# Loading the value weights whole and first, and making three pairs of values before the queries and keys of step 0

## The chip, the cores and the metric

The kernel runs on one core of a Trainium2 chip. The metric is the device time of one execution in microseconds (us). The engines are TensorE (PE, with its weight loads shown apart as PEld), VectorE (DVE), ScalarE (ACT), GpSimd (POOL) and SyncE (SP). SP computes nothing here: it issues most of the DMAs, in the order of the program. All DMAs are carried by the same 16 DMA engines.

## The reference

Four blocks follow each other, each on a layer norm of the 2048 x 512 input and added to it: attention with a recurrent memory (A), a dense block (B), A again, B again. Everything is bfloat16.

```python
def _A_ref(x, mem0, Wq, Wk, Wv, Wo, seg_len):   # seg_len 32, M = 8 memory rows, H = 32 heads of 128
    mem = mem0
    for s in range(n_seg):                      # 64 segments
        h = jnp.concatenate([mem, xs], axis=1)  # 8 memory rows + 32 tokens
        q, k, v = (jnp.einsum('btd,dhe->bhte', h, W) for W in (Wq, Wk, Wv))
        scores = jnp.where(mask, jnp.einsum('bhqe,bhke->bhqk', q, k) * scale, -1e9)
        o = jnp.einsum('bhqk,bhke->bhqe', _softmax(scores), v)
        o = jnp.einsum('bhte,hed->btd', o, Wo)
        mem = o[:, :M, :]                       # the next segment's memory
        outs.append(o[:, M:, :])
def _B_ref(x, w1, w2):                          # 512 -> 1376 -> 512
    return jnp.maximum(x @ w1, 0) @ w2
x = x + _A_ref(_layernorm(x), ...); x = x + _B_ref(_layernorm(x), ...)   # and both once more
```

The memory rows make the segments a chain: a segment needs the output of the one before it.

## The kernel before

**Steps.** The kernel runs 68 steps. Step k does segment k of the first attention and, four steps behind it, segment k - 4 of the second one; the dense blocks of earlier segments run beside them. Steps 0 to 3 have the first attention alone. Inside a step the 32 heads are done in two halves of 16: queries and keys (`qk`, in batches of 6, 6 and 4 heads), scores, softmax; then the probabilities are turned, the values are weighted (`weighted_v`), and the output product with Wo gives the new memory rows (`output_mem`, `new_memory`), with which the next step starts.

**Order.** The instructions of PE, DVE, SP and POOL run in the order in which the program emits them (a manual schedule); ACT's order is chosen by the framework. An instruction that waits therefore holds everything behind it on its engine.

**Head.** Before the steps, `load_xb(0)` and the weights are issued on SP. Each of Wq, Wk and Wv (4.19 MB, 128 partitions x 4 x 4096 columns) comes in two halves of 2.1 MB, one for each half of the heads, by `load_w`: x0, Wq first half, mem0, x1, Wk first half, Wv first half, and then in `load_rest` x2, the three second halves, Wo in five parts (4.19 MB) and x3. `xbs[n]` holds 128 rows of input. Its layer norm is `moments_x` (statistics on DVE, the power on POOL) and `normalize` (DVE); `inputs_T(n)` turns it with four PE transposes into a PSUM tile and copies that to `xT0[n]` with ACT. `tokens_in` puts the tokens of a step into `HT` (the moving or stationary operand of all products), and a copy on POOL puts the tokens of a step into `HTm`, beside the memory rows.

**Values.** There are four kinds. `values_first(ii)` gives the values of segment 0's memory and tokens: for each half of the heads two PSUM tiles of eight matmuls, the first copied to `Vs` by ACT, the second by DVE, two copies each. `memory_values` makes the values of the memory rows (and of 16 rows of a later segment that ride along), `values_second` those of segment 1, and `values0(p, n)` those of the pair of segments 2 and 3 of every 128 input rows (p odd; n = 0, 2, 4, 6 stand for a quarter of the heads each): eight matmuls into one PSUM tile, an ACT copy to a staging tile, a store to DRAM by SP, from where a later step loads them. In step 0 the staging tiles are slices (`slots`) of the buffers that will hold the dense weights.

The PSUM tiles of `values_first`, `values_second`, `values0` and of the transposes come from one pool of two buffers (`ps_fill`); queries, keys, memory values and turned probabilities share three buffers (`ps_c`). So a tile can be started when the tile two (or three) before it has been copied out.

**Step 0 (`first_step`).** It does the first half of the heads, then values (first half of `values_first`, `memory_values`, `values_second`, and four groups of `values0` for pairs 1 and 3, with the layer norm and transposes of x2 between), then the second half of the heads with two groups of pair 5 between, the second half of the values, and the output, among whose five parts five more groups of `values0` are spread. Groups that are left go into steps 1 (three), 2 (one) and 4 (one) by `values_at`; from step 5 on another rule holds, the same in both kernels.

**Names in the profile.** L241 transposes, L591 queries and keys, L597 and L599 their copies by ACT and DVE, L625 scores, L643 to L664 softmax, L329 `values_first`, L334 its copies, L797 memory values, L354 second values, L310 `values0`, L320 its copy, L232 to L227 the layer norm of an input, L675 turning of probabilities, L701 weighted values, L719 their copies, L633 output product of the memory rows, L849 to L872 the new memory.

Of the kernel before, what the change touches and what calls it, by code (L numbers as in the profile page):

```python
# [7 lines left out]
BF = mybir.dt.bfloat16  # L8
# [14 lines left out]
def kernel(  # L23
# [14 lines left out]
    nc = tc.nc  # L38
# [62 lines left out]
    nc.vector.memset(mem0[:], 0.0)  # L101
    xbs = {}

    def load_xb(n):
        tag, bufs = ("vst", 5) if n in (1, 2, 3) else ("xb", 1)
        xbs[n] = wk.tile([128, Dm], BF, tag=tag, bufs=bufs, name="xb")
        nc.sync.dma_start(out=xbs[n][:], in_=A_x[0, 128 * n:128 * n + 128, :])

    load_xb(0)
    R_tiles = {}  # L110

    def residual(d):
# [17 lines left out]
    PW = H * Dh // 2  # L130
    WO_PARTS = ((0, 8), (8, 16), (16, 24), (24, 28), (28, 32))

    def load_w(W_sb, W_v, pc):
        nc.sync.dma_start(out=W_sb[:, :, pc * PW:(pc + 1) * PW], in_=W_v[:, :, pc * PW:(pc + 1) * PW])

    load_w(Wq_sb, Wq_v, 0)
    nc.sync.dma_start(out=mem0[0:M, :], in_=A_mem0[0, :, :])
    load_xb(1)
    load_w(Wk_sb, Wk_v, 0)
    load_w(Wv_sb, Wv_v, 0)  # L140

    def load_rest():
        load_xb(2)
        load_w(Wq_sb, Wq_v, 1)
        load_w(Wk_sb, Wk_v, 1)
        load_w(Wv_sb, Wv_v, 1)
# [432 lines left out]

    def qk_batch(n, h0, nh, a_lo, a_hi, between=None):
        ncol = (a_hi - a_lo) * L
        res = {}

        for W_sb, nm in (((Wq_sb, "QT"), (Wk_sb, "KT")) if n < 2 else ((Wk_sb, "KT"), (Wq_sb, "QT"))):
            qp = ps_c.tile([128, HB, 2 * L], F32, tag="c")
            for hi in range(nh):
                h = h0 + hi
                for c4 in range(NC4):  # L590
                    nc.tensor.matmul(qp[:, hi, 0:ncol], lhsT=W_sb[:, c4, h * Dh:(h + 1) * Dh],  # L591
                                     rhs=HT[:, c4, a_lo:a_hi, :], start=(c4 == 0), stop=(c4 == NC4 - 1))
            dst = wk.tile([128, nh, 2 * L], BF, tag=f"{nm}{n}", bufs=1, name=nm)
            if nm == "QT":
                if between:
                    between()
                nc.scalar.copy(out=dst[:, 0:nh, a_lo * L:a_hi * L], in_=qp[:, 0:nh, 0:ncol])  # L597
            else:
                nc.vector.tensor_copy(out=dst[:, 0:nh, a_lo * L:a_hi * L], in_=qp[:, 0:nh, 0:ncol])  # L599
            res[nm] = dst  # L600
        return res["QT"], res["KT"]

    BATCHES = ((0, 6), (6, 6), (12, 4))

    def qk(hf, act, between=None, behind=None):
        res = []
        for n, (o, nh) in enumerate(BATCHES):
            res.append((o, nh) + qk_batch(n, 16 * hf + o, nh, act[0], act[-1] + 1, None if n else between))
# [7 lines left out]
        for a in act:  # L616
            nc.vector.tensor_copy(out=sp_tiles[a], in_=maskb2)  # L617

    def scores(qks, act):
        for a in act:  # L620
            sp = sp_tiles[a]
# [13 lines left out]

    last_exp = [None]

    def exponentials(act):
        mxs, ess = {}, {}
        for a in act:  # L640
            sp = sp_tiles[a]
            mxs[a] = wk.tile([128, 8], F32, tag="mx", bufs=2, name="mx")
            nc.vector.tensor_reduce(out=mxs[a][:], in_=sp, axis=AX.X, op=ALU.max)  # L643
        for a in act:
            sp = sp_tiles[a]
# [166 lines left out]
    def block(k, lo, hi):  # L812
        output_x(k - 1, lo, hi)
        groups = values_at(k)
        if split(k):

            rest = [(i, 0, NC4) for i in range(1, len(groups))]
            if k == 1:
                todo = [] if lo == 0 else [(0, 0, 2)] if hi == 16 else [(0, 2, NC4)] + rest
            else:  # L820
                todo = [(0, 0, 2)] if lo == 0 else [(0, 2, NC4)] if hi == 16 else rest
        elif k < 5:
            todo = [(0, 0, NC4)] if k == 4 and lo else []
# [11 lines left out]
    def values_at(k):  # L835


        if k < 5:
            return {1: [(5, 6), (7, 0), (7, 2)], 2: [(7, 4)], 4: [(7, 6)]}.get(k, [])
        if k % 4 != 1 or not has0(k + 1):  # L840
            return []
        groups = [(p, n) for p in range(9, NSEG // 2, 2) for n in range(0, NCH, 2)]
        i = k // 4 - 1
        lo = 3 * min(i, 12) + 4 * max(i - 12, 0)
        return groups[lo:lo + (3 if i < 12 else 4)]
# [39 lines left out]
    def first_step():  # L885


        slots = iter([w1_flat[:, 512 * i:512 * i + 512] for i in range(NC4 * Dff // 512)] +
                     [w2_flat[:, 512 * i:512 * i + 512] for i in range(8)])
        masks(0)  # L890
        with tc.high_priority(offset=PRIO):
            qks = qk(0, [0])
            scores(qks, [0])
            softmax(0, [0], True)
            values_first(0)
            memory_values(0, (next(slots), None), (0,))
            values_second(0, next(slots))
            values0(1, 0, stage=next(slots))
            values0(1, 2, stage=next(slots))
            m = moments_x(2)  # L900
            normalize(nc.vector, xbs[2], xbs[2], m, 0, 128)
            inputs_T(2)
            values0(3, 0, stage=next(slots))
            values0(3, 2, stage=next(slots))
            load_x(1)
            qks = qk(1, [0], between=lambda: values0(5, 0, stage=next(slots)))
            scores(qks, [0])
            softmax(1, [0], True)
            values0(5, 2, stage=next(slots))
            values_first(1)  # L910
            memory_values(0, (None, next(slots)), (1,))
            transpose_p(1)
            tokens_in(1)
            nc.gpsimd.tensor_copy(out=HTm[:, :, 2 * M:32], in_=spare_T(1))
            values_second(1, next(slots))
            pvs = weighted_v([0])
            outputs(0, pvs)
            wo = ps_wo.tile([128, Dm], F32, tag="wo", name="wo")
            for groups, heads in zip((((1, 4),), ((1, 6),), ((3, 4),), ((3, 6), (5, 4)), ()), WO_PARTS):
                for p, n in groups:  # L920
                    values0(p, n, stage=next(slots))
                output_mem(0, wo, *heads)
            new_memory(0, [0], wo)
            output_ride(0)
            prepare(1)
# [225 lines left out]
```

## Time and profile before

| | us |
|---|---|
| median of 3 runs | 1581.19 (1581.16 to 1582.31) |
| the profiled execution | 1581.75 |
| its span | 1580.0 |
| PE busy | 1548.6 (98%) |
| DVE busy | 1277.3 (81%) |
| ACT busy | 734.7 (47%) |
| POOL busy | 349.8 (22%) |
| first matmul of a query | 16.61 after the span's start |
| first matmul of step 1's queries | 51.20 after the span's start |

The span runs from the first to the last instruction of the program; the execution's own time has some 1.7 us around it. "Busy" is the union of the instructions' times on an engine; times in the timeline count from the span's start.

### The profile page before, as it was taken

The page shows a single profiled execution, that of the slowest core. Times are in us where ns is not written, and L with a number is a line of the kernel's source. Part 1 is how long each engine was busy: PE and PEld are TensorE (multiplying, and loading weights), DVE is VectorE, ACT ScalarE, POOL GpSimd, SP SyncE. Part 2 cuts the span into 40 slices and gives each one's busy share as a digit, 9 for nine tenths or more (in the row PEclk, how much of TensorE's full clock was granted, in tenths as well). Part 3 has the DMA queues.
Part 4 walks back from the last instruction along what each step waited for, and adds up shares of the span by engine and source line. Part 5 has one row for each costly group of instructions (what it writes and reads, how often), then busy time and mean ns, then how long its engine had stood idle before and what let it go on. Part 6 is the DMA issues. An engine that isn't in the chain of part 4 may idle for free. (4 is left out here: it accounts for less than half of the span.)

```text
span 1580.0 us, 95139 instructions
## 1 busy us (share of the span) xinstructions
PE 1548.6 (98%) x42866; PEld 1286.3 (81%) x42866; DVE 1277.3 (81%) x3300; ACT 734.7 (47%) x1762; POOL 349.8 (22%) x670
## 2 busy tenths in 40 slices
PE   5899999999999999999999999999999999999998
PEld 3677888888888888888888888988888898888876
DVE  3578888888888888888888888888888888887866
ACT  3435445454544545454454545445454544545433
POOL 2012122222222222222122222212222221222110
PEclk9999999999999999999999999999999999999999
DMA  9734432434353244434433343443443344333331
GB/s 369 246 77 76 87 84 78 81 92 79 78 92 84 78 82 94 80 76 91 84 80 80 99 80 76 88 84 79 77 99 77 72 87 80 82 74 95 75 69 41
DMA packets 222021, 146.26 MB, mean 93 GB/s; under 512 B 123464, under 2 KB 215984, under 8 KB 221616
## 3 DMA queue, kind: packets, MB, share of 16 engines
q1 hardware_dynamic: 218448, 135.96, 38.8%
q8 instruction: 336, 5.51, 1.5%
q0 software_dynamic: 3072, 4.20, 1.1%
q14 instruction: 69, 0.57, 0.1%
q10 hardware_dynamic: 96, 0.03, 0.0%
HBM read 65.41 MB, written 45.35 MB: 70 GB/s over the span
## 5 line engine op out<-in xcount | busy, mean ns | idle before, releaser
L597 ACT CAST QT<-qp 128x480 bf16<-128x480 f32 (+3 forms) x408 | 201.5, 494 | 433.4 <-PE qp L591 433.1
L591 PE MATMUL qp<-HT,Wq_sb 128*128 128x80 bf16 (+1 forms) x8704 | 371.3, 200 | 3.2 <-POOL HT L786 1.2
L591 PEld LDWEIGHTS <-Wq_sb 128*128 128x128 bf16 x8704 | 325.9, 100 | 35.2 <-issue 27.5
L591 PE MATMUL qp<-HT,Wk_sb 128*128 128x80 bf16 (+1 forms) x8704 | 347.3, 199 | 1.7 <-issue 1.3
L591 PEld LDWEIGHTS <-Wk_sb 128*128 128x128 bf16 x8704 | 319.5, 100 | 2.6 <-issue 1.6
L664 POOL TENSOR_TENSOR P_sb<-es,sm 128x320 bf16<-128x320 f32 x185 | 130.8, 721 | 714.8 <-ACT QT L597 299.4
L599 DVE CAST KT<-qp 128x480 bf16<-128x480 f32 (+3 forms) x408 | 220.3, 565 | 36.3 <-PE qp L591 32.9
L643 DVE TENSOR_REDUCE mx<-sp 128x8 f32<-128x320 f32 x256 | 115.1, 487 | 133.1 <-PE sp L625 130.9
L373 PE MATMUL wox<-Wo_sb,OTx 128*64 128x256 bf16 x2880 | 173.6, 273 | 0.0
L373 PEld LDWEIGHTS <-OTx 128*64 128x64 bf16 x2880 | 150.2, 110 | 2.9
L649 ACT ACTIVATE es<-es 128x320 f32<-128x320 f32 x256 | 109.5, 468 | 61.9 <-DVE es L647 61.0
L797 PE MATMUL vm<-Wv_sb,HTm 128*32 128x512 bf16 x2176 | 129.4, 379 | 1.8 <-DVE KT L599 1.0
L354 PE MATMUL v<-Wv_sb,xnT 128*32 128x512 bf16 x2048 | 128.8, 378 | 0.0
L633 PE MATMUL wo<-Wo_sb,OTm 128*32 128x512 bf16 x2144 | 128.6, 380 | 0.0
L659 DVE TENSOR_REDUCE sm<-es 128x8 f32<-128x320 f32 x256 | 117.4, 459 | 13.5 <-ACT es L649 5.0
L617 DVE CAST sp<-maskb 128x320 f32<-128x320 bf16 x256 | 118.3, 483 | 0.0
L647 DVE TENSOR_TENSOR es<-sp,mx 128x320 f32<-128x320 f32 x256 | 113.6, 482 | 1.5
L543 PE MATMUL sp<-w_sb,hT 128*64 128x256 bf16 (+4 forms) x1452 | 103.9, 276 | 0.4 <-issue 0.4
L522 PE MATMUL hp<-xnT,w_sb 128*128 128x64 bf16 (+1 forms) x2948 | 98.5, 192 | 0.9 <-issue 0.5
L801 ACT CAST VmS<-vm 128x512 bf16<-128x512 f32 x134 | 78.5, 586 | 44.4 <-PE vm L797 42.5
L222 POOL TENSOR_TENSOR mv<-mv,mhalf_t 128x1 f32<-128x1 f32 x82 | 45.8, 558 | 224.6 <-DVE mv L221 218.9
L797 PEld LDWEIGHTS <-HTm 128*32 128x32 bf16 x2176 | 54.7, 97 | 48.8 <-issue 3.1
(125 smaller groups left out, 2088.5 us busy)
## 6 DMA issues: line engine op xcount, KB each, us to landing
Vs<-vd SPq DMA_DIRECT2D x96, 256.0 KB
vd<-vst SPq DMA_DIRECT2D x181, 128.0 KB
vmd<-VmS SPq DMA_DIRECT2D x134, 128.0 KB
Vs<-vmd SPq DMA_DIRECT2D x254, 32.0 KB
Vs<-vmd SPq DMA_DIRECT2D x60, 128.0 KB
Wq_sb<-in_A_Wq_dram SPq DMA_DIRECT2D x2, 2048.0 KB
Wk_sb<-in_A_Wk_dram SPq DMA_DIRECT2D x2, 2048.0 KB
Wv_sb<-in_A_Wv_dram SPq DMA_DIRECT2D x2, 2048.0 KB
```

The lines of the kernel that those rows point to most:

```text
L354: nc.tensor.matmul(vp[32 * j:32 * j + 32, :], lhsT=tokens[:, c4, :], rhs=Wv_sb[:, c4, n * 512:(n + 1) * 512], start=(c4 == 0), stop=(c4 == ...
L373: nc.tensor.matmul(out[64 * j:64 * j + nr, 0:256], lhsT=lhsT, rhs=rhs[:, 256 * j:256 * j + 256], start=start, stop=stop, tile_position=(0, ...
L591: nc.tensor.matmul(qp[:, hi, 0:ncol], lhsT=W_sb[:, c4, h * Dh:(h + 1) * Dh], rhs=HT[:, c4, a_lo:a_hi, :], start=(c4 == 0), stop=(c4 == NC4 ...
L597: nc.scalar.copy(out=dst[:, 0:nh, a_lo * L:a_hi * L], in_=qp[:, 0:nh, 0:ncol])
L599: nc.vector.tensor_copy(out=dst[:, 0:nh, a_lo * L:a_hi * L], in_=qp[:, 0:nh, 0:ncol])
L617: nc.vector.tensor_copy(out=sp_tiles[a], in_=maskb2)
L633: nc.tensor.matmul(wo[32 * j:32 * j + 32, :], lhsT=OTm[:, h, n, 2 * M * c:2 * M * c + 4 * M], rhs=Wo_sb[:, h, :], start=(h < 4), stop=(h > ...
L643: nc.vector.tensor_reduce(out=mxs[a][:], in_=sp, axis=AX.X, op=ALU.max)
L647: nc.vector.tensor_tensor(out=es[:], in0=sp, in1=mxs[a][:].unsqueeze(2).to_broadcast([128, 8, L]), op=ALU.subtract)
L659: nc.vector.tensor_reduce(out=sm[:], in_=es[:], axis=AX.X, op=ALU.add)
L664: eng.tensor_tensor(out=P, in0=es[:], in1=sm[:].unsqueeze(2).to_broadcast([128, 8, L]), op=ALU.mult)
L797: nc.tensor.matmul(vp[32 * j:32 * j + 32, :], lhsT=HTm[:, c4, :], rhs=Wv_sb[:, c4, n * 512:(n + 1) * 512], start=(c4 == 0), stop=(c4 == NC ...
```

## The change

Wv is loaded by one DMA of 4.19 MB, the first on SP. x0 and mem0 are issued on ACT's queue instead of SP's. `load_rest` issues x1, x2, then Wq and Wk with one DMA each, then Wo and x3 as before. In the head, x0 is normalized ahead of the turning of mem0, and x1 and x2 are normalized after `tokens_in(0)`, ahead of the whole of step 0; their transposes stand inside it.

Step 0 has a new order on PE: all of `values_first`, the transposes of x1 and x2, memory values, second values, two groups of pair 1, the first half's queries, two groups of pair 1, the second half's queries, the four groups of pair 3, two groups of pair 5, then keys and scores of the first half, keys and scores of the second half, each half's softmax behind the other's keys, one group of pair 5 before the probabilities are turned, and the last group of pair 5 in the middle of the output product. Each half of the heads has a score bank of its own, and the masks that the setup put there are used, so `masks` is called no more in step 0. `qk_batch` is split into `qk_part`, which makes queries or keys alone. The second half's queries are held in three of the slots. Step 0 now makes 12 groups of `values0`, one more than before; steps 1 and 2 make as many as before, each of a later index, and step 4 makes none.

The diff, without what only follows from it:

```diff
-    def load_xb(n):
+    def load_xb(n, queue=nc.sync):
...
-        nc.sync.dma_start(out=xbs[n][:], in_=A_x[0, 128 * n:128 * n + 128, :])
-
-    load_xb(0)
+        queue.dma_start(out=xbs[n][:], in_=A_x[0, 128 * n:128 * n + 128, :])
+
+    load_xb(0, nc.scalar)
...
-    load_w(Wq_sb, Wq_v, 0)
-    nc.sync.dma_start(out=mem0[0:M, :], in_=A_mem0[0, :, :])
-    load_xb(1)
-    load_w(Wk_sb, Wk_v, 0)
-    load_w(Wv_sb, Wv_v, 0)
+
+    nc.sync.dma_start(out=Wv_sb[:], in_=Wv_v)
+    nc.scalar.dma_start(out=mem0[0:M, :], in_=A_mem0[0, :, :])
 
     def load_rest():
+        load_xb(1)
         load_xb(2)
-        load_w(Wq_sb, Wq_v, 1)
-        load_w(Wk_sb, Wk_v, 1)
-        load_w(Wv_sb, Wv_v, 1)
+        nc.sync.dma_start(out=Wq_sb[:], in_=Wq_v)
+        nc.sync.dma_start(out=Wk_sb[:], in_=Wk_v)
...
+    def qk_part(nm, n, h0, nh, a_lo, a_hi, between=None, dst=None):
         ncol = (a_hi - a_lo) * L
+        W_sb = Wq_sb if nm == "QT" else Wk_sb
+        qp = ps_c.tile([128, HB, 2 * L], F32, tag="c", name="qp")
+        for hi in range(nh):
+            h = h0 + hi
+            for c4 in range(NC4):
+                nc.tensor.matmul(qp[:, hi, 0:ncol], lhsT=W_sb[:, c4, h * Dh:(h + 1) * Dh],
+                                 rhs=HT[:, c4, a_lo:a_hi, :], start=(c4 == 0), stop=(c4 == NC4 - 1))
+        if dst is None:
             dst = wk.tile([128, nh, 2 * L], BF, tag=f"{nm}{n}", bufs=1, name=nm)
+        if between:
+            between()
+        copy = nc.scalar.copy if nm == "QT" else nc.vector.tensor_copy
+        copy(out=dst[:, 0:nh, a_lo * L:a_hi * L], in_=qp[:, 0:nh, 0:ncol])
+        return dst
...
-            todo = [(0, 0, NC4)] if k == 4 and lo else []
+            todo = []
...
-            return {1: [(5, 6), (7, 0), (7, 2)], 2: [(7, 4)], 4: [(7, 6)]}.get(k, [])
+            return {1: [(7, 0), (7, 2), (7, 4)], 2: [(7, 6)]}.get(k, [])
...
-        masks(0)
...
+            for ii in range(2):
+                values_first(ii)
+            for n in (1, 2):
+                inputs_T(n)
+            nc.gpsimd.tensor_copy(out=HTm[:, :, 2 * M:32], in_=spare_T(0))
+            memory_values(0, (next(slots), next(slots)))
+            for ii in range(2):
+                values_second(ii, next(slots))
             load_x(1)
+            for n in (0, 2):
+                values0(1, n, stage=next(slots))
+            q0 = queries(0, [None] * len(BATCHES))
+            for n in (4, 6):
+                values0(1, n, stage=next(slots))
+            q1 = queries(1, [next(slots)[:, 0:nh * L].rearrange("p (h q) -> p h q", h=nh) for _, nh in BATCHES])
+            for n in range(0, NCH, 2):
+                values0(3, n, stage=next(slots))
+            for n in (0, 2):
+                values0(5, n, stage=next(slots))
+            scores(with_heads(q0, keys(0)), [0])
+            ess = exponentials([0])
+            scores(with_heads(q1, keys(1)), [0], sp_tiles[1:])
+            softmax(0, [0], True, ess)
+            ess = exponentials([0], sp_tiles[1:])
+            values0(5, 4, stage=next(slots))
+            softmax(1, [0], True, ess)
             transpose_p(1)
             tokens_in(1)
             nc.gpsimd.tensor_copy(out=HTm[:, :, 2 * M:32], in_=spare_T(1))
-            values_second(1, next(slots))
             pvs = weighted_v([0])
             outputs(0, pvs)
             wo = ps_wo.tile([128, Dm], F32, tag="wo", name="wo")
...
+            for part, (h0, h1) in enumerate(WO_PARTS):
+                if part == 2:
+                    values0(5, 6, stage=next(slots))
+                output_mem(0, wo, h0, h1)
...
         load_rest()
+
+        def normalize_xb(n):
+            normalize(nc.vector, xbs[n], xbs[n], moments_x(n), 0, 128)
+
+        normalize_xb(0)
         tp = transpose_pe(mem0)
...
-        for n in range(2):
-            m = moments_x(n)
-            normalize(nc.vector, xbs[n], xbs[n], m, 0, 128)
-            inputs_T(n)
+        inputs_T(0)
         load_x(0)
-        nc.gpsimd.tensor_copy(out=HTm[:, :, 2 * M:32], in_=spare_T(0))
         tokens_in(0)
+        for n in (1, 2):
+            normalize_xb(n)
         first_step()
```

More of the change, by code (lines that the diff above doesn't have):

```diff
@@ L129 @@
     Wo_v = A_Wo.rearrange("h e d -> e h d")
-    PW = H * Dh // 2
     WO_PARTS = ((0, 8), (8, 16), (16, 24), (24, 28), (28, 32))
-    def load_w(W_sb, W_v, pc):
-        nc.sync.dma_start(out=W_sb[:, :, pc * PW:(pc + 1) * PW], in_=W_v[:, :, pc * PW:(pc + 1) * PW])
-    load_w(Wq_sb, Wq_v, 0)
-    nc.sync.dma_start(out=mem0[0:M, :], in_=A_mem0[0, :, :])
-    load_xb(1)
-    load_w(Wk_sb, Wk_v, 0)
-    load_w(Wv_sb, Wv_v, 0)
+    nc.sync.dma_start(out=Wv_sb[:], in_=Wv_v)
+    nc.scalar.dma_start(out=mem0[0:M, :], in_=A_mem0[0, :, :])
     def load_rest():
+        load_xb(1)
         load_xb(2)
-        load_w(Wq_sb, Wq_v, 1)
-        load_w(Wk_sb, Wk_v, 1)
-        load_w(Wv_sb, Wv_v, 1)
+        nc.sync.dma_start(out=Wq_sb[:], in_=Wq_v)
+        nc.sync.dma_start(out=Wk_sb[:], in_=Wk_v)
         for h0, h1 in WO_PARTS:
@@ L578, in store @@
             nc.sync.dma_start(out=out[0, SEG * g:SEG * g + SEG, :], in_=ob[r:r + SEG, :])
-    def qk_batch(n, h0, nh, a_lo, a_hi, between=None):
+    def qk_part(nm, n, h0, nh, a_lo, a_hi, between=None, dst=None):
         ncol = (a_hi - a_lo) * L
[L584 to L592, printed above, removed]
-            dst = wk.tile([128, nh, 2 * L], BF, tag=f"{nm}{n}", bufs=1, name=nm)
[L594 to L600, printed above, removed]
+        W_sb = Wq_sb if nm == "QT" else Wk_sb
[6 more added lines that the diff above has]
+        if dst is None:
+            dst = wk.tile([128, nh, 2 * L], BF, tag=f"{nm}{n}", bufs=1, name=nm)
+        if between:
[3 more added lines that the diff above has]
+        return dst
@@ L601, in qk_batch, with qk @@
+    def qk_batch(n, h0, nh, a_lo, a_hi):
+        res = {nm: qk_part(nm, n, h0, nh, a_lo, a_hi) for nm in (("QT", "KT") if n < 2 else ("KT", "QT"))}
         return res["QT"], res["KT"]
     BATCHES = ((0, 6), (6, 6), (12, 4))
-    def qk(hf, act, between=None, behind=None):
+    def qk(hf, act, behind=None):
         res = []
         for n, (o, nh) in enumerate(BATCHES):
-            res.append((o, nh) + qk_batch(n, 16 * hf + o, nh, act[0], act[-1] + 1, None if n else between))
+            res.append((o, nh) + qk_batch(n, 16 * hf + o, nh, act[0], act[-1] + 1))
@@ L617, in masks, with scores @@
             nc.vector.tensor_copy(out=sp_tiles[a], in_=maskb2)
-    def scores(qks, act):
+    def scores(qks, act, banks=sp_tiles):
         for a in act:
-            sp = sp_tiles[a]
+            sp = banks[a]
             for o, nh, QT, KT in qks:
@@ L636, with exponentials @@
     last_exp = [None]
-    def exponentials(act):
+    def exponentials(act, banks=sp_tiles):
         mxs, ess = {}, {}
         for a in act:
-            sp = sp_tiles[a]
+            sp = banks[a]
             mxs[a] = wk.tile([128, 8], F32, tag="mx", bufs=2, name="mx")
@@ L644, in exponentials @@
         for a in act:
-            sp = sp_tiles[a]
+            sp = banks[a]
             es = ess[a] = wk.tile([128, 8, L], F32, tag="es", bufs=2, name="es")
@@ L888, in first_step @@
         slots = iter([w1_flat[:, 512 * i:512 * i + 512] for i in range(NC4 * Dff // 512)] +
-                     [w2_flat[:, 512 * i:512 * i + 512] for i in range(8)])
-        masks(0)
-        with tc.high_priority(offset=PRIO):
[L892 to L904, printed above, removed]
-            load_x(1)
[L906 to L911, printed above, removed]
+                     [w2_flat[:, 512 * i:512 * i + 512] for i in range(NFC)])
@@ new lines, in keys, with queries, with_heads @@
+        def keys(hf):
+            return [qk_part("KT", n, 16 * hf + o, nh, 0, 1) for n, (o, nh) in enumerate(BATCHES)]
+        def queries(hf, dst):
+            return [qk_part("QT", n, 16 * hf + o, nh, 0, 1, dst=dst[n]) for n, (o, nh) in enumerate(BATCHES)]
+        def with_heads(QTs, KTs):
+            return [(o, nh, Q, K) for (o, nh), Q, K in zip(BATCHES, QTs, KTs)]
+        with tc.high_priority(offset=PRIO):
+            for ii in range(2):
[6 more added lines that the diff above has]
+                values_second(ii, next(slots))
+            load_x(1)
+            for n in (0, 2):
[15 more added lines that the diff above has]
+            softmax(1, [0], True, ess)
@@ L918, in first_step @@
             wo = ps_wo.tile([128, Dm], F32, tag="wo", name="wo")
[L919 to L922, printed above, removed]
+            for part, (h0, h1) in enumerate(WO_PARTS):
+                if part == 2:
+                    values0(5, 6, stage=next(slots))
+                output_mem(0, wo, h0, h1)
             new_memory(0, [0], wo)
```

## The prediction

> **What bounds the kernel now.** I read the page first, then the busy time by stretches of the first 50 us, then the timeline of that part, and last the timeline of step 4, the only later step that the change alters in amount.
>
> ```profile
> span 1580.0 us, 95139 instructions
> PE 1548.6 (98%) x42866; PEld 1286.3 (81%) x42866; DVE 1277.3 (81%) x3300; ACT 734.7 (47%) x1762; POOL 349.8 (22%) x670
> ```
>
> PE is the bound of the whole, so whatever delays PE's entry into step 1 shifts the end one for one, and a matmul group taken out of a full step gives its time back. The stretches (PE, PEld, DVE, ACT, POOL busy with counts, granted clock, DMA share, GB/s) show the one part where PE is not full:
>
> ```profile
> 0.00:10.00 10.00, 1.25 (x6) 0.55 (x6) 2.27 (x7) 1.28 (x1) 7.16 (x23) 1.00 0.78 294
> 10.00:20.00 10.00, 4.63 (x111) 4.18 (x111) 3.92 (x14) 1.89 (x4) 2.31 (x5) 1.00 1.04 398
> 20.00:30.00 10.00, 9.12 (x132) 5.08 (x128) 5.53 (x13) 5.22 (x10) 1.11 (x2) 1.00 1.03 410
> 30.00:40.00 10.00, 8.99 (x208) 5.98 (x208) 4.53 (x11) 4.82 (x11) 0.29 (x1) 1.00 1.05 374
> 40.00:50.00 10.00, 9.71 (x144) 4.06 (x136) 2.72 (x9) 5.36 (x12) 0.24 (x1) 1.00 1.07 345
> ```
>
> The DMA engines are full up to 50 us: 16.8 MB of attention weights and a little input come in one stream. The timeline (start, length, engine, line, tiles, count, idle time before and what ended it):
>
> ```profile
> 4.59 0.69 PE L213 MATMUL sp<-maskb,ident 128*128 128x320 bf16 x2 [4.59 <-POOL maskb L175]
> ...
> 9.44 0.59 PE L241 MATMUL tpx<-ident,mem 128*128 128x128 bf16 x4 [4.16 <-DMA mem<-in_A_mem_dram]
> ...
> 12.49 0.69 DVE L232 BATCH_NORM_STATS2 stats<-xb 128x6 f32<-128x512 bf16 x1
> ...
> 14.33 0.41 DVE L227 TENSOR_SCALAR xb<-xb,mv 128x512 bf16<-128x512 bf16 x1 [0.74 <-POOL mv L222]
> ...
> 16.61 0.96 PE L591 MATMUL qp<-HT,Wq_sb 128*128 128x40 bf16 x24 [1.20 <-POOL HT L786]
> 17.40 0.97 PE L591 MATMUL qp<-HT,Wk_sb 128*128 128x40 bf16 x24
> ...
> 21.49 1.89 PE L329 MATMUL vf<-Wv_sb,HT 128*40 128x512 bf16 x16
> ...
> 24.40 1.38 DVE L334 CAST Vs<-vf 40x512 bf16<-40x512 f32 x2
> ...
> 32.35 0.77 PE L591 MATMUL qp<-HT,Wk_sb 128*128 128x40 bf16 x24 [0.32 <-DMA Wk_sb<-in_A_Wk_dram]
> 32.96 0.75 PE L591 MATMUL qp<-HT,Wq_sb 128*128 128x40 bf16 x24
> ...
> 37.52 1.91 PE L329 MATMUL vf<-Wv_sb,HT 128*40 128x512 bf16 x16 [0.58 <-DMA Wv_sb<-in_A_Wv_dram]
> ...
> 49.06 0.65 PE L633 MATMUL wo<-Wo_sb,OTm 128*32 128x512 bf16 x8
> ...
> 51.20 0.77 PE L591 MATMUL qp<-HT,Wq_sb 128*128 128x40 bf16 x24 [0.47 <-DVE HT L872]
> ```
>
> PE has its first real work at 16.61, waits for Wk at 32.35 and for Wv at 37.52, ends step 0's output at 49.71 and starts step 1 at 51.20. So step 0 follows the stream closely; its end cannot move forward much, because Wo's 4.19 MB come last: from 37.52 at about 349 GB/s that is 49.5.
>
> In step 4:
>
> ```profile
> 126.52 1.05 PE L310 MATMUL vp<-Wv_sb,xT 128*64 128x512 bf16 x8
> ...
> 127.51 1.19 PE L543 MATMUL sp<-w_sb,hT 128*32 128x320 bf16 x18
> ```
>
> **The change, part by part.**
>
> *Arrivals.* Before, mem0 came at 9.4 behind x0 and half of Wq, 2.24 MB. The same 16 engines now carry x0, mem0 and all of Wv, 2.10 MB more: at 398 to 422 GB/s 5.0 to 5.3 us, so 14.5; Wv is issued first (at 0.81 instead of 1.27), which may give 0.4 back. I take W = 14.3, between 14.0 and 14.8. x1 follows 0.3 later. Wk is now the last of the first 12.98 MB, where the second half of Wv was, so it comes at 37.5; Wq comes at about W + 11.5 = 25.8. Whether 8 KB rows run faster than 4 KB rows the trace does not show; the stretches bound the stream between 374 and 410 GB/s, single microseconds up to 426.
>
> *x0 and mem0 on ACT's queue.* Two issues of some 0.4 us ahead of a table load that ended at 2.09 and is wanted first at about 10. x0's statistics still wait on POOL, whose power stands behind memsets until 8.26; after that 0.56 + 0.41 + 0.60 + 0.59 + 0.28 give step 0's HT at about 11, over 3 us ahead of W. Cost nothing; if x0 came at over 9 us it would begin to.
>
> *The new wait on DVE.* `normalize_xb(1)` and `(2)` now stand on DVE ahead of all of step 0, and both inputs are behind Wv. One such chain takes 2.25 us (12.49 to 14.74, with the power on POOL inside). DVE is free at 14.6 + 4.5 = 19.1. Behind it stand the two copies of `values_first`'s second tile, 1.38 us, to 20.5. That pool has two buffers, so the fourth tile cannot start before 20.5; its own DVE copies hold x2's transposes to 21.5 + 1.4 = 22.9. Before, each of these copies had other PE work over it. PE is through the transposes at 23.2, 8.9 us after W, for about 4 us of matmuls.
>
> *PE up to the keys.* Two back-to-back groups of eight value matmuls take 1.73 (1.92 less a 0.19 tail), and a change of kind 0.1. From 23.2: memory values and second values, 3.7; two groups, 1.85; queries, 64 x 25 ns + 0.1 = 1.7 (25 ns from 32.35 to 32.96 for 24); two groups, 1.85; queries, 1.7; six groups, 5.3. That is 16.1, so keys start at K = 39.3. Wq and Wk are there by then: PE, not the stream, is now late, by 1.8 us.
>
> *From the keys to step 1.* The two softmaxes now have two value groups beside them, where before values of the other half filled the gaps. I follow DVE in its order from K: first keys on PE and their last copy 2.15, scores 0.25; maximum and subtraction 1.0; three key copies 1.15; sum, reciprocal, product 1.24; second maximum and subtraction 1.0, exponential 0.55 with the turned-P copy beside it; sum, reciprocal, product 1.24: 8.6. Transposes 0.55, copy 0.5, and the first weighted values' copies 0.5: output starts at K + 10.2. Heads 0 to 15, 1.1; value group (5, 6), 0.95; the other heads, 1.15: K + 13.4 = 52.7, with Wo's last part there by 49.5. The 1.49 us from there to step 1 (49.71 to 51.20) stay: 54.2 instead of 51.2, **+3.0**. I allow 1 us either way.
>
> *Later steps.* Steps 1 and 2 still compute three and one groups, one index later each. Step 4 loses its only group, 126.52 to 127.51, in a stretch where PE is full: **-0.99**. If the softmax chain of that step were late instead, it would be 0. Stores: SP issues the stores of step 0 behind the weights in both kernels; the first load behind them (second values) has until the weighted values of step 1, ten microseconds later. The two masks taken out of step 0 (0.48 each) were not on PE's path.
>
> *Sum.* +3.0 - 0.99 = **+2.0 us**. The profiled execution took 1581.75 for a span of 1580.0; it becomes 1583.75. It was 0.56 above the median of 1581.19, so on the median **1583.2**, 0.13% above.
>
> *A pace that the granted clock does not show.* The clock column says 1.00 throughout, yet 24 query matmuls take 0.80 us at 16.6 and 0.60 at 32.4, and a pair of 320-column products at 4.59 starts 0.26 us apart, where 512 columns take 0.216 later: half speed. The slow pace lasted from 16.61 to about 20.9. Now it falls on the wide value products. In my sum that costs nothing, since the first two tiles are done before 19.1 even at half speed. [...]
>
> **The rivals.**
>
> *B, the slow pace outlasts the waits, slower.* If PE's first burst (14.3 to 19) does not release it, or the thin work up to 23 loses it, the fourth tile takes 0.87 more and some 4.3 us after 23.2 run at half speed, 2.1 lost: +5.0, **1586.2**. For it: 4.2 us of unbroken work were needed before. Against: waits of 1 us in step 1 brought no slow pace back. It decides over 0.2% once the loss is above 1.2 us.
>
> *C, DVE does not hold PE, not slower.* If the inputs were normalized beside the first values, PE would need 20.2 us and 2.1 for the slow pace from W: 36.6, ahead of Wk. Then K = 37.5, step 1 at 52.4: +1.2 - 0.99, **1581.4**. Only with the stream at 422 GB/s all along besides would it be below before, about 1580.5. Against it: DVE's order is written out, x1 can't come before Wv, and Wo's arrival forbids more.
>
> **How the numbers follow.** 0.2%, about what a measurement of this kernel can tell from no change, is 3.16 us: 1578.0 to 1584.4. Forecast 0.55, of which 0.13 lies above 1584.4 by its own 1 us on the chain and 0.5 on W; B 0.30, of which 0.27 is above; C 0.15, of which 0.03 is faster. So slower 0.40, same 0.57, faster 0.03. Range 1580.9 to 1586.6: C's middle and B's middle with some room.
>
> **What would show it.** Right: first `vf` matmul near 14.3; the DVE normalizations of x1 and x2 ending near 19, the fourth `vf` tile waiting for a DVE copy; first Wk matmul near 39.3 without a wait for a DMA; two idle stretches of PE around the second softmax, 2 us or more; step 1 at 54; step 4 one microsecond shorter. Wrong if keys wait for Wk (C), if value groups of eight take 1.7 us after 23 (B), or if step 1 starts before 52.

## The result, and the profile after

| | us |
|---|---|
| median before, measured together | 1581.66 (1581.16 to 1582.31, 6 runs) |
| median after | 1592.28 (1589.54 to 1594.64, 6 runs) |
| ratio | 1.0066 [1.0053, 1.0079] |
| the profiled execution after | 1593.29, span 1591.6, mean granted clock 0.997 |

The change makes the kernel 0.66% slower, some 10.6 us, where 2.0 were forecast: outside the range, and with the sign on the side that had 0.40. The page first: the same work, and PE still busy for 98%, but in a span 11.6 us longer.

```profile
span 1591.6 us, 95129 instructions
PE 1552.9 (98%) x42866; PEld 1288.7 (81%) x42866; DVE 1276.7 (80%) x3298; ACT 734.6 (46%) x1762; POOL 349.7 (22%) x670
```

The stretches that were shown of before (length, then busy time and count of PE, PEld, DVE, ACT, POOL; granted clock, DMA share, GB/s):

```profile
10.00:20.00 10.00, 4.78 (x27) 2.21 (x28) 4.08 (x10) 2.91 (x5) 1.40 (x3) 1.00 1.04 412
20.00:30.00 10.00, 9.33 (x166) 5.32 (x167) 1.38 (x2) 5.70 (x11) 0.72 (x2) 1.00 1.02 412
30.00:40.00 10.00, 10.00 (x193) 6.60 (x189) 0.75 (x2) 5.70 (x11) 0.00 (x0) 1.00 1.05 376
40.00:50.00 10.00, 5.42 (x131) 4.12 (x132) 6.12 (x16) 1.75 (x4) 0.47 (x2) 0.76 1.03 333
50.00:60.00 10.00, 8.84 (x191) 5.08 (x188) 4.20 (x15) 2.90 (x9) 0.00 (x0) 0.73 0.41 134
```

Up to 40 us PE is as full as the forecast had it. Between 40 and 50 us it works 5.42 of 10 us, and the granted clock falls: 0.76, then 0.73, in a column that said 1.00 all along before. The timeline of the same part (start, length, engine, line, tiles, count, idle time before and what ended it; `values_first` is now L323, its copies L328, the transposes L235, the layer norm L221, queries and keys L583, scores L620, `values0` L304, the turning of probabilities L670, the output product L628):

```profile
13.97 4.68 PE L323 MATMUL vf<-Wv_sb,HT 128*40 128x512 bf16 x24 [3.96 <-DMA Wv_sb<-in_A_Wv_dram]
19.92 1.04 PE L323 MATMUL vf<-Wv_sb,HT 128*40 128x512 bf16 x8 [1.26 <-ACT Vs L328]
...
21.97 0.38 PE L235 MATMUL tpx<-ident,xb 128*128 128x128 bf16 x4 [0.67 <-ACT xT L242]
```

```profile
18.28 0.41 DVE L221 TENSOR_SCALAR xb<-xb,mv 128x512 bf16<-128x512 bf16 x1 [0.73 <-POOL mv L216]
18.60 1.38 DVE L328 CAST Vs<-vf 40x512 bf16<-40x512 f32 x2
18.70 1.18 ACT L328 CAST Vs<-vf 40x512 bf16<-40x512 f32 x2 [1.62 <-PE vf L323]
```

```profile
38.25 1.77 PE L583 MATMUL qp<-HT,Wk_sb 128*128 128x40 bf16 x64
39.95 0.71 PE L620 MATMUL sp<-KT,QT 128*40 128x40 bf16 x16
40.59 1.77 PE L583 MATMUL qp<-HT,Wk_sb 128*128 128x40 bf16 x64
42.29 0.42 PE L620 MATMUL sp<-KT,w_sb 128*40 128x40 bf16 x12
45.10 0.23 PE L620 MATMUL sp<-KT,w_sb 128*40 128x40 bf16 x4 [2.39 <-issue]
45.15 1.90 PE L304 MATMUL vp<-Wv_sb,xT 128*64 128x512 bf16 x8
46.81 0.78 PE L670 MATMUL tp<-ident,P_sb 128*64 128x80 bf16 x16
49.71 0.74 PE L670 MATMUL tp<-ident,P_sb 128*64 128x80 bf16 x16 [2.12 <-DVE P_sb L659]
...
53.41 1.92 PE L304 MATMUL vp<-Wv_sb,xT 128*64 128x512 bf16 x8
55.25 1.11 PE L628 MATMUL wo<-Wo_sb,OTm 128*32 128x512 bf16 x16
...
57.87 0.77 PE L583 MATMUL qp<-HT,Wq_sb 128*128 128x40 bf16 x24 [0.47 <-DVE HT L867]
```

Two things stand here that no step of the prediction has. First, the second half's 16 scores break off after 12 and go on 2.39 us later, ended by "issue": PE waited for no result of any engine and no transfer that the profile knows. Second, a group of eight value matmuls lasts 1.90 at 45.15 and 1.92 at 53.41, where one took 1.05 before (at 42.62): half speed, from 45.2 to 55.4 by the clock's record, which is 10.24 us long. The shortest record of half clock in these runs is 3.41 us long (48.1 to 51.5 in the first experiment); that length is called a window here, so these are three. Step 1 starts at 57.87 instead of 51.20, 6.67 later.

In stretches of 4 us, from 38 on:

```profile
38.00:42.00 4.00, 3.93 (x140) 3.51 (x137) 2.40 (x6) 0.92 (x3) 0.00 (x0) 1.00 1.10 348
42.00:46.00 4.00, 1.61 (x37) 1.04 (x35) 2.42 (x8) 0.22 (x1) 0.47 (x2) 0.90 1.09 349
46.00:50.00 4.00, 1.88 (x32) 1.29 (x30) 2.05 (x5) 1.28 (x3) 0.00 (x0) 0.50 0.92 309
50.00:54.00 4.00, 4.00 (x66) 2.22 (x64) 1.90 (x7) 1.11 (x4) 0.00 (x0) 0.50 0.69 231
```

PE works 1.61 of 4 us while the DMA engines are full (share 1.09, 349 GB/s); the clock then falls to half and stays there although PE is full again from 50.

### The profile page after: what moved, and what is told of

Read it like the earlier page. It is cut to its first block, busy times and chain, and to the rows that moved or that the text cites. A ratio compares the mean times of both kernels' runs of the same rounds, so it can differ in the third digit from the quotient of the medians.

```text
span 1591.6 us, 95129 instructions
## 1 busy us (share of the span) xinstructions
PE 1552.9 (98%) x42866; PEld 1288.7 (81%) x42866; DVE 1276.7 (80%) x3298; ACT 734.6 (46%) x1762; POOL 349.7 (22%) x670
## 3 DMA queue, kind: packets, MB, share of 16 engines
q8 instruction: 336, 5.51, 1.5%
## 5 line engine op out<-in xcount | busy, mean ns | idle before, releaser
L583 PE MATMUL qp<-HT,Wq_sb 128*128 128x80 bf16 (+1 forms) x8704 | 370.7, 199 | 4.4 <-issue 3.5
L583 PEld LDWEIGHTS <-Wq_sb 128*128 128x128 bf16 x8704 | 325.0, 99 | 36.5 <-issue 29.1
L583 PE MATMUL qp<-HT,Wk_sb 128*128 128x80 bf16 (+1 forms) x8704 | 346.2, 199 | 2.0 <-issue 2.0
L583 PEld LDWEIGHTS <-Wk_sb 128*128 128x128 bf16 x8704 | 318.7, 99 | 2.9 <-issue 2.8
L628 PE MATMUL wo<-Wo_sb,OTm 128*32 128x512 bf16 x2144 | 129.1, 382 | 0.0
L216 POOL TENSOR_TENSOR mv<-mv,mhalf_t 128x1 f32<-128x1 f32 x82 | 45.7, 558 | 220.0 <-DVE mv L215 219.9
L792 PEld LDWEIGHTS <-HTm 128*32 128x32 bf16 x2176 | 55.0, 97 | 48.1 <-issue 2.3
```

The lines of the kernel that those rows point to most:

```text
L628: nc.tensor.matmul(wo[32 * j:32 * j + 32, :], lhsT=OTm[:, h, n, 2 * M * c:2 * M * c + 4 * M], rhs=Wo_sb[:, h, :], start=(h < 4), stop=(h > ...
L792: nc.tensor.matmul(vp[32 * j:32 * j + 32, :], lhsT=HTm[:, c4, :], rhs=Wv_sb[:, c4, n * 512:(n + 1) * 512], start=(c4 == 0), stop=(c4 == NC ...
```

## The experiments

The runs were made on several chips. Each ratio is against runs of the kernel before on the same chip in the same session, whose medians were 1581.36 to 1583.60 us, so compare the ratios rather than the times. Each run has one trace.

**The theories.** *Blocks*: PE's instructions reach it by DMA, on the queue that the page's third part calls instruction:

```profile
q8 instruction: 336, 5.51, 1.5%
```

336 packets of 5.51 MB are 16 KB each; PE has 2 x 42,866 matmuls and weight loads, 255 for each packet. By this estimate a packet is a block of some 128 matmuls with their loads. The change puts 160 narrow matmuls (keys and scores) back to back while the weights fill the DMA engines (share 1.10 from 38 to 42 us). Taking the stop (at matmul 478, counted from the start) for a block border, the border before it, 350, is reached at 38.97, the stop at 42.71, and PE goes on at 45.10, 6.1 us after the first; an instruction packet's transfer began at 42.42. These 128 narrow matmuls took 3.7 us. In the kernel before, wide work stood between these borders (34.26 and 41.40), and PE did not wait at the second one. *Clock*: the half clock is what makes the loss large, and the waits bring it on: the stop, the second softmax, or both. *Order*: the stop is a wait of the new order itself (scores for copies) that the trace names wrongly; it then stays wherever the borders fall.

**Moving the borders by 64 matmuls.** 64 products of 40 columns that nothing reads, before the turning of mem0, where PE waits for Wv anyway.

```diff
         normalize_xb(0)
+        idle = ps_fill.tile([128, Dm], F32, tag="fill", name="idle")
+        for i in range(64):
+            nc.tensor.matmul(idle[:, 0:L], lhsT=ident[:], rhs=maskb[:], start=True, stop=True)
         tp = transpose_pe(mem0)
```

> 64 products of 128x40 that nobody reads, put on PE while it waits for the weights, move every later matmul 64 places down the instruction stream. Theory F (PE's instructions come in blocks of 128 matmuls; a block asked for while the DMA engines are full takes about 6 us; 128 narrow matmuls last only 4, so PE ran dry for 2.39 us at matmul 478, and the thin stretch brought the half clock from 45.2 to 55.4): the block border now falls among wide value products, the 2.39 us stop in the second scores is gone, the clock stays at 1.00, step 1 starts at 53 to 54.5 instead of 57.9, and the time falls by 3 to 5 us, to about 1588. Theory S (the waits for the two softmaxes alone bring the half clock): the stop may go, the clock still falls near 45 to 49 us, step 1 at 55.5 or later, time 1590 to 1592.

Measured: 1586.26 us, ratio 1.0025 [1.0009, 1.0041]. The stop is gone: all 16 scores in one piece.

```profile
42.07 0.71 PE L620 MATMUL sp<-KT,w_sb 128*40 128x40 bf16 x16
42.61 1.05 PE L304 MATMUL vp<-Wv_sb,xT 128*64 128x512 bf16 x8
43.72 0.48 PE L670 MATMUL tp<-ident,P_sb 128*64 128x80 bf16 x16
46.43 0.48 PE L670 MATMUL tp<-ident,P_sb 128*64 128x80 bf16 x16 [2.23 <-DVE P_sb L659]
...
49.61 1.92 PE L304 MATMUL vp<-Wv_sb,xT 128*64 128x512 bf16 x8
...
54.02 0.77 PE L583 MATMUL qp<-HT,Wq_sb 128*128 128x40 bf16 x24 [0.47 <-DVE HT L867]
```

The wait for the second softmax (2.23 us) is left, and with it one stretch of half clock, 48.1 to 51.5, on the output product, where theory F had expected none. Step 1 starts at 54.02. Two of the six executions took 1591 us.

**Moving them by 128.** The same edit with `range(128)`: one whole block, so that the borders fall on the same matmuls again.

> The same with 128 dead products, a whole block, so that the borders fall where they did. Theory F: the stop of about 2.4 us in the second scores and the half clock stay, step 1 near 58, time as the changed kernel (1590 to 1594). If the dead products helped only because they keep PE awake early, this one would be as fast as the one with 64. Theory S: as the changed kernel too.

Measured: 1595.09 us, ratio 1.0074 [1.0059, 1.0089]. The stop is back, on the same four scores, now at matmul 606 = 478 + 128:

```profile
44.03 0.42 PE L620 MATMUL sp<-KT,w_sb 128*40 128x40 bf16 x12
46.79 0.26 PE L620 MATMUL sp<-KT,w_sb 128*40 128x40 bf16 x4 [2.34 <-issue]
```

The half clock lasts from 46.1 to 56.3, and this profile has it in front too, 12.0 to 18.8: behind the added products the speed was full early (the four transposes of x0 take 0.40 us at 9.41, where they take 0.61 in the changed kernel), and during the wait for Wv, 5.79 us here, it was half again. Wv came at 15.60 in this trace, 1.6 us later than in the changed kernel's, which is part of the higher time of this execution. So the stop goes with the number of instructions ahead, not with the order: the order theory is out.

**Wide products among the narrow ones.** Nothing added; the two groups of pair 5 that stood ahead of the keys go between keys and scores.

```diff
-            for n in (0, 2):
-                values0(5, n, stage=next(slots))
-            scores(with_heads(q0, keys(0)), [0])
+            k0 = keys(0)
+            values0(5, 0, stage=next(slots))
+            scores(with_heads(q0, k0), [0])
...
-            scores(with_heads(q1, keys(1)), [0], sp_tiles[1:])
+            k1 = keys(1)
+            values0(5, 2, stage=next(slots))
+            scores(with_heads(q1, k1), [0], sp_tiles[1:])
```

> Value groups (5, 0) and (5, 2) stand between the keys and the scores of each half instead of ahead of the keys. Theory F: the narrow run gets 1.8 us longer, the stop shrinks to about 1 us or less, and the clock holds or falls for fewer windows; keys start near 37.5 with the arrival of Wk; step 1 at 53 to 55, time 1586 to 1590. Theory S: the groups cover copies, not the softmax, so the clock falls all the same; step 1 at 56 to 57, time 1590 to 1592.

Measured: 1589.49 us, ratio 1.0038 [1.0021, 1.0055]. The idle time ahead of the last four scores shrinks to 1.36 us, and they start 6.0 us behind the block border ahead of them (40.04 to 46.05), as in the changed kernel (6.1), but in the profiled execution step 1 starts at 58.12, which is a miss: the clock was at half from 22.8 to 26.2, so the keys came at 38.92, and again from 50.1 to 56.9, over the whole output product. (The trace puts the 1.36 down to `P_sb`, which scores do not read; the matmul is the same fourth from the end.)

```profile
46.05 0.23 PE L620 MATMUL sp<-KT,w_sb 128*40 128x40 bf16 x4 [1.36 <-DVE P_sb L659]
```

**Step 4's group back in its place.** `values_at` and the rest of step 4 as before, and no group (5, 6) in step 0.

```diff
-            todo = []
+            todo = [(0, 0, NC4)] if k == 4 and lo else []
...
-            return {1: [(7, 0), (7, 2), (7, 4)], 2: [(7, 6)]}.get(k, [])
+            return {1: [(5, 6), (7, 0), (7, 2)], 2: [(7, 4)], 4: [(7, 6)]}.get(k, [])
...
-                if part == 2:
-                    values0(5, 6, stage=next(slots))
```

> Undoes one part: step 0 makes 11 groups again and steps 1, 2 and 4 make the groups they made before. By my sum step 0 gets 0.95 us shorter at full clock (1.9 at half) and step 4 0.99 longer, so no difference beyond 1 us. If what step 4 lost in work it gave back in waits for its instructions (0.78 and 0.47 us at matmuls 2650 and 2776 in the changed kernel's trace), step 4 does not get longer, and this kernel is 1 to 2 us faster than the changed one: 1590 to 1591.

Measured: 1590.19 us, ratio 1.0047 [1.0032, 1.0062]; the stop is there (2.31 us), and so is the half clock (45.7 to 56.0). From one new memory product to the next, step 4 takes 23.52 us with its group, 24.35 in the changed kernel without it, 24.08 before: taking the group out saved nothing that these traces show. The timelines of step 4 say why: PE has "issue" waits there as well, in the kernel before (first two lines) and in the changed one (the others).

```profile
121.62 0.30 PE L591 MATMUL qp<-HT,Wk_sb 128*128 128x80 bf16 x4 [0.23 <-issue]
...
125.35 1.24 PE L401 MATMUL wox<-Wo_sb,OTx 128*32 128x128 bf16 x76 [0.70 <-issue]
```

```profile
129.36 0.60 PE L583 MATMUL qp<-HT,Wk_sb 128*128 128x80 bf16 x12 [0.61 <-issue]
...
133.36 1.36 PE L395 MATMUL wox<-Wo_sb,OTx 128*32 128x128 bf16 x84 [0.78 <-issue]
...
137.34 0.43 PE L696 MATMUL pv<-PT,Vs 40*128 40x40 bf16 x21 [0.47 <-issue]
```

The first two of each kernel lie at matmuls 2522 and 2650, the third at 2776, again some 128 apart. In this run one such wait is left in step 4, 0.52 us at matmul 2650.

**Both kernels again, unchanged, on one chip.**

> The kernel before, unchanged, as a run of its own, so that its trace comes from the same chip as the next ones. Open is the part of the loss that grows after step 5 (3.6 us in the changed kernel's trace, 0.5 with 64 dead products, 4.6 to 6.9 in the other three), where both kernels execute the same stream. If that part belongs to the chip or the execution, this trace shows waits for instructions too and the time spreads over 1581 to 1587; if it belongs to the change, this one has none: 1581 to 1583.

> The changed kernel, unchanged, on the same chip. Theory F: step 0 again with a stop of 2.3 to 2.4 us at matmul 478 and three windows of half clock; 6 to 7 us at step 0, 7.5 to 8 us at step 5 against the trace of before from this chip, and the rest as that part turns out: 1590 to 1594.

Measured: before 1581.99 us (ratio to the common runs of before 1.0001 [0.9993, 1.001]); after 1590.78, ratio 1.0061 [1.0046, 1.0076]. The stop repeats (2.27 us), with half clock from 47.1 to 54.0, two windows instead of three. Against the trace of before from the same chip, step 1 starts 5.5 us later (57.07 against 51.59) and step 5 5.7 us later, less than the 6 to 7 and 7.5 to 8 that were expected. From step 5 to the end the changed kernel loses another 0.5 us here and 3.7 in the first pair of traces; the kernel before, traced again, moves by up to 2.7 us against its own first trace on the way. Waits ended by "issue" are in both kernels: they add up to 4.1 and 3.6 us in the two traces of before, and to 10.5 and 7.5 in those of the changed kernel, the stop included. Behind step 5 alone they are 1.6 and 2.8 against 4.2 and 3.4. So most of what the first pair loses there, 2.6 of 3.7 us, is again this wait, which differs from one execution of a kernel to the next; that it is the change's is not shown.

**The DMA engines freed.** Wo and x3 are issued behind the stores of step 0 instead of ahead of the steps; nothing else changes.

```diff
         nc.sync.dma_start(out=Wk_sb[:], in_=Wk_v)
+    def load_wo():
         for h0, h1 in WO_PARTS:
...
             softmax(1, [0], True, ess)
+            load_wo()
             transpose_p(1)
```

> The changed kernel with the DMAs of Wo and x3 issued behind the store of value group (5, 4), so that the 16 DMA engines carry next to nothing between Wk's arrival (37.5) and about 47. Step 0 must then wait for Wo, to 58 or later. Theory F (the block of instructions comes late because the DMA engines are full): the stop at matmul 478 in the second scores falls to under 0.8 us, as in the unloaded later steps, and the clock does not fall at 45. If the stop stays at 2.4, the full DMA engines are not its cause. Time 1594 to 1602, by the wait for Wo.

Measured: 1593.27 us, a single execution, just below the range that was expected. Stretches and timeline of this run (its lines are one higher):

```profile
38.00:42.00 4.00, 3.93 (x146) 3.73 (x144) 2.68 (x7) 1.06 (x2) 0.00 (x0) 1.00 0.50 160
42.00:46.00 4.00, 2.01 (x44) 1.12 (x40) 3.69 (x11) 1.38 (x3) 0.47 (x2) 1.00 0.31 54
```

```profile
42.01 0.71 PE L621 MATMUL sp<-KT,w_sb 128*40 128x40 bf16 x16
...
50.73 1.05 PE L629 MATMUL wo<-Wo_sb,OTm 128*32 128x512 bf16 x8 [2.94 <-DMA Wo_sb<-in_A_Wo_dram]
```

With the DMA engines at 0.50 and 0.31 instead of 1.10 and 1.09, the same border at the same matmul costs nothing (0.07 us). The block's packet starts 0.37 us behind the border ahead of it (38.69), where it started 3.45 us behind in the changed kernel. The run as a whole gains nothing, as Wo now comes late (2.94, 1.97, 0.45 and 0.83 us of waits, and half clock from 48.2 to 65.2).

**Filling the waits with the work that is there.** 64 products as in the first experiment; group (5, 0) between the first keys and scores, (5, 2) and (5, 4) behind the second scores, and (5, 6) moved from the output product to the wait for the second softmax.

```diff
-            for n in (0, 2):
-                values0(5, n, stage=next(slots))
-            scores(with_heads(q0, keys(0)), [0])
+            k0 = keys(0)
+            values0(5, 0, stage=next(slots))
+            scores(with_heads(q0, k0), [0])
             ess = exponentials([0])
             scores(with_heads(q1, keys(1)), [0], sp_tiles[1:])
+            values0(5, 2, stage=next(slots))
...
             softmax(1, [0], True, ess)
+            values0(5, 6, stage=next(slots))
             transpose_p(1)
```

> 64 dead products as before, and the value groups of pair 5 dealt out over the waits: (5, 0) between the first keys and scores, (5, 2) and (5, 4) behind the second scores, (5, 6) between the two turnings of probabilities instead of inside the output product. Theory F with a smaller share for the softmax waits (they alone brought one window of half clock at 48.1 with 64 dead products): no stop, no half clock, keys at about 37.5 with Wk, step 1 at 51.5 to 53; time between 0 and 3 us above the kernel before on this chip. Theory S: the clock still falls once, step 1 at 53.5 to 54.5, 3 to 5 us above.

Measured: 1584.25 us, ratio 1.0012 [1.0004, 1.0021]. Step 1 starts at 51.93 and step 0 has no half clock in this profile (it has one such stretch at 1572, in the tail). Two short waits for instructions are left in step 0, 0.39 us in the second keys and 0.21 in the weighted values, where none was expected. But 7 of the 11 runs, not six as the text of a later experiment says, have a mean clock of 0.995 to 0.998: it falls in runs that were not traced.

**Only the clock.** The first experiment, and nine products of 512 columns that nothing reads in the wait for the second softmax.

```diff
             softmax(1, [0], True, ess)
+            idle = ps_wo.tile([128, Dm], F32, tag="wo", name="idle")
+            for i in range(9):
+                nc.tensor.matmul(idle[:], lhsT=ident[:], rhs=Wv_sb[:, i % NC4, 0:512], start=True, stop=True)
             transpose_p(1)
```

> The kernel with 64 dead products, and nine dead products of 512 columns more in the 2.23 us that PE waits for the second softmax between the two turnings of probabilities. With 64 alone the clock was halved from 48.1 to 51.5 and step 1 came at 54.0. If that wait alone brings the window (the part of theory S that is left), the clock now stays at 1.00 through step 0, step 1 comes at 52.0 to 53.0, and the median falls by 1 to 2 us against 64 alone, to 2 us or less above the kernel before on this chip. If the window comes from the stretch before (42 to 45, scores and one value group), it stays: 54.0 and 2.5 to 4 us above.

Measured: 1581.49 us, ratio 0.9995 [0.9986, 1.0004]. PE waits for the second softmax as long as before, but with work in its hands, and the groups behind it run at full speed:

```profile
44.52 1.89 PE L924 MATMUL idle<-Wv_sb,ident 128*128 128x512 bf16 x8 [0.16 <-issue]
...
49.26 1.05 PE L304 MATMUL vp<-Wv_sb,xT 128*64 128x512 bf16 x8
...
52.79 0.77 PE L583 MATMUL qp<-HT,Wq_sb 128*128 128x40 bf16 x24 [0.47 <-DVE HT L867]
```

So that one wait had brought the first experiment's stretch of half clock. (The trace's mean clock of 0.997 comes from elsewhere: half clock at 10.8 to 17.6, during and behind the wait for Wv, and at 1570.6 to 1574.1.) Step 4 takes 23.11 us here, with 0.49 us of waits for instructions. That is 0.97 less than in the first trace of the kernel before, but no less than the 23.12 of its second trace, so it does not show the gain that the prediction had put down.

**Filled and awake.** The filled kernel with products of 512 columns in three waits: five ahead of the fourth tile of `values_first`, two between the transposes of x1 and x2, three before the second turning.

```diff
+            if n == 6:
+                idle = ps_wo.tile([128, Dm], F32, tag="wo", name="idle")
+                for i in range(5):
+                    nc.tensor.matmul(idle[:], lhsT=ident[:], rhs=Wv_sb[:, i % NC4, 0:512], start=True, stop=True)
             vp = ps_fill.tile([128, 512], F32, tag="fill", name="vf")
```

> The kernel with the groups of pair 5 dealt out, and dead products of 512 columns in its other waits of step 0: five ahead of the fourth tile of the first values, two between the transposes of x1 and x2, three ahead of the second turning. Six of eleven executions of the one without them had a mean granted clock of 0.995 to 0.998. If the half clock there came from the thin stretches at 19 to 23 and 46, the clock is now 0.999 or 1.000 in nearly all, and the median falls by 1 to 2 us, to within 1.5 us of the kernel before; step 1 at 51.5 to 52. If it comes from the end of the kernel (1572 to 1575 in the trace), nothing changes: 1.5 to 3 us above.

Measured: 1579.26 us, ratio 0.9981 [0.9973, 0.999]; 9 of the 11 runs have a mean clock of 0.999 or 1.000. Its stretch from 40 to 50 us, beside 5.42 and 0.76 in the changed kernel:

```profile
40.00:50.00 10.00, 9.42 (x220) 6.20 (x217) 7.36 (x21) 4.60 (x12) 0.47 (x2) 1.00 1.01 328
```

**Is that a gain over before?** The same kernel once more, and beside it the kernel before with 74 products ahead of the turning of mem0, as the filled kernel has 64 and ten more, to see whether moved borders alone bring something.

> The kernel with dealt out groups and dead products once more, beside the control on the same chip: 0.997 to 0.999 of the kernel before again, step 1 at 51 to 52, clock 1.00 through step 0.

> The kernel before with 74 dead products of 128x40 on PE ahead of the turning of mem0, as many dead products as the kernel with dealt out groups and dead products has, so that its blocks of instructions have the same borders against the later steps. That kernel was 0.9981 of the kernel before. If its gain comes from the moved borders alone, this one gains as much: 0.997 to 0.999. If it comes from the order of step 0 and the group taken out of step 4, this one is within 0.1% of the kernel before.

Measured: the filled and awake kernel 1581.84 us, ratio 0.9995 [0.9986, 1.0004]; before with moved borders 1581.42, ratio 0.9996 [0.9987, 1.0005]. The borders alone bring nothing to the kernel before. Of the best version it can be said that it undoes the loss; whether it is 0.2% ahead of before stays open, as one measurement says so and the other does not.

## Why the prediction was wrong

**What held.** Wv's wait ended at 13.97 (14.3 said), the layer norm of x2 ended at 18.69 (19.1), the fourth tile started at 19.92 (20.5), and the keys at 38.25 without a wait for a DMA (39.3). Of the two idle stretches foreseen around the second softmax one was there, 2.12 us; the other, 2.39 us, was the stop for instructions and went with it.

**Right in time, wrong in mechanism: "the new wait on DVE".** The fourth tile was to wait for DVE's copies of the second one, behind the layer norms. The lines above name ACT: its copies of the third tile end at 19.87, PE starts at 19.92, and DVE's copies of the second end only at 19.98. x2's transposes likewise waited 0.67 us for ACT's copy of x1's, not for DVE's copies of the fourth tile. ACT is named for the fourth tile in every trace with this order but the one with 128 products, where DVE ended last, by 0.46 us. So a tile does not always wait for the one two before it, and in the others DVE did not hold PE there. The sum had a wait of about the right size for another reason: that part is luck. Rival C's condition, that DVE does not hold PE, was met; its numbers were not, as the keys came at 38.25 and not at 37.5 with Wk.

**The step that failed: "from the keys to step 1".** The output product was to end 13.4 us after K; it ends 18.1 after (38.25 to 56.36). The terms were durations of work at full clock with PE's instructions always at hand, and neither holds in that place. With both put right, the output ends 13.1 us after the keys (38.20 to 51.29 with the clock held), so the sum itself was good to 0.3; with the keys 1.1 earlier than said, +3.0 becomes the +1.6 of the table's second row. The three profiles split the 6.67 us by which step 1 is late:

| start of step 1's queries | us | what is added |
|---|---|---|
| before | 51.20 | |
| borders moved, clock held awake | 52.79 | +1.59, the new order itself |
| borders moved | 54.02 | +1.23, half clock after the softmax wait |
| the changed kernel | 57.87 | +3.85, the stop of 2.39 and two more windows of half clock |

Each row is one trace. The second traces of the kernel before and of the changed one have 51.59 and 57.07, so the parts are good to some 0.4 to 0.8 us. That the row with borders moved alone agrees with the forecast 54.2 is chance: it is the order with 1.6 instead of 3.0, and 1.2 of half clock.

**Later steps: -0.99 did not come.** The work did get shorter: without its waits, step 4 is 23.1 us long in both traces of the kernel before and 22.3 in both of the changed one, 0.8 less. But with them it takes 24.08 and 23.12 before, 24.35 and 23.55 after, since waits for instructions (0.61, 0.78 and 0.47 in the first trace) took the room. The prediction called PE full in that stretch; the step had such waits before the change too (0.23 and 0.70 in the first trace, none in the second). It allowed for 0, but by a late softmax.

**Rival B had the mechanism in the wrong place.** It let the half clock come from the thin work in front, up to 23 us, and priced it at +5.0. That thin work brings it was an estimate: the trace of before has no half clock between 20.9 us and the end of its span. The profile after has full-speed groups there from 17.9 on, and half speed from 45.2. One trace does have B's place, that with wide products among the narrow ones, which is the same up to the keys: half clock from 22.8 to 26.2, and keys 0.7 later. The prediction also took the clock column as blind to the slow pace; it shows it, 0.76 and 0.73, once the clock has had its first record (20.9 us in the trace of before; up to there the column prints 1.00). The price of a wait was put at its own length, and no step asked what PE's share falls to around it: 1.61 of 4 us.

**What stays open.** Up to step 1 the traces lose 5.5 to 6.7 us; the medians differ by 8.8 to 10.6. Mean clocks of 0.995 to 0.998 in the runs of the changed kernel allow at most 3 to 8 us of lost clock (1592 times 0.002 to 0.005), so some runs had more half clock than the traced ones, which lost 3.4 and 5.1. Where, the runs without a trace don't say. Behind step 5 the waits for instructions differ from execution to execution; what sets them there was not followed further.

## What to carry to other kernels

Before wide filler work is moved ahead of a dependent chain, ask which waits it was covering. Here 128 narrow matmuls back to back lasted 3.7 us, and PE went on 6.1 us behind their start while the weights filled the DMA engines (share 1.10); wide products among them shrank the stop from 2.39 to 1.36 us. The wait of 2.2 us for the second softmax cost its own length and another 1.2 us of half clock behind it; nine products that nothing reads, put into the wait, kept the clock up and brought step 1 from 54.02 to 52.79. An "issue" wait on PE of 2.39 us was gone with 64 matmuls more ahead of it and back, as 2.34 on the same four scores, with 128: so it was told from a wait of the order itself.

## What the runs showed of the hardware

**The stops and the DMA engines.** The page has 336 packets of 16 KB on an instruction queue, by the estimate above some 128 pairs of matmul and weight load each. In step 0, with the DMA engines full (1.10 and 1.09 in the changed kernel), PE went on 6.0 to 6.1 us behind the border before in the five traces of the new order with a stop of over 1 us; with the engines at 0.50 and 0.31, in one execution, after 3.8 us with next to no wait (0.07). That is no constant of full engines: in the kernel before with 74 products it was 4.0 us, with a wait of 0.43 and the engines at 1.03. Nor do full engines explain every wait: the five of 0.23 to 0.78 in step 4 of the first traces came with a DMA share of 0.04 to 0.73 in the 4 us up to their ends.

**The clock fell behind stretches in which PE was not idle throughout.** The records of half clock inside the span are 3.41, 6.83, 10.24 and, with Wo late, 17.07 us long: about one, two, three and five times the shortest. In the 3.41 us before the fall at 45.2 PE was at work for 1.02 us (30%); before the fall at 48.1 in the first experiment, which has the softmax wait of 2.23 us alone, for 1.61 (47%); with products in that wait PE was at work for 3.17 of 3.40 at the same place, and the clock stayed. Other falls came behind 40% (47.1, second trace of the changed kernel), 52% (46.1, with 128 products), 40% (50.1, with wide products among the narrow ones) and 42% (48.2, with Wo late). It stayed at 1.00 in the kernel before, where no 3.41 us between 21 and 60 us have PE at work for less than 66%, and behind 60% near the end of the changed one (1581.2 to 1584.6). At what share it falls these traces do not show.
